# Turning normed tokens by VectorE pieces and DRAM transfers in place of TensorE identity products, in an adaLN + S4 convolution + SwiGLU kernel

## The chip, the cores and the metric

The kernel runs on one core of a Trainium2 chip. The metric is device time in microseconds (us), the median of several runs. One execution is also recorded by the hardware profiler; its rows are what this document calls the profile or the trace, and its times count from the first instruction of that execution.

The core has five engines that each work through their own list of instructions in order: TensorE (PE in the rows; PEld is its weight load), VectorE (DVE), ScalarE (ACT), GpSimd (POOL) and SyncE (SP, which here only issues DMAs). They wait for one another by semaphores. SBUF is the on-chip memory, PSUM the memory that matmuls write.

## The reference, cut to what matters

Input: 2048 tokens of width D = 448, as 16 tiles of 128 tokens.

```python
sa, ca, ga, sb, cb, gb = (silu(c) @ w_mod).reshape(6, D)
h = layernorm(x) * (1 + ca) + sa
x = x + ga * (S4_convolution(h) + h * Dskip)      # along the tokens
h = layernorm(x) * (1 + cb) + sb
x = x + gb * ((silu(h @ w_gate) * (h @ w_up)) @ w_down)   # inner width 1792
```

All of it is in float32. The second layernorm, its modulation by cb and sb, and the fact that `h @ w_gate` contracts over the 448 features are what the change touches: tokens lie on the partitions when they are normed, and features must lie on the partitions when they are multiplied.

## The kernel before, in words

The tokens are taken in six blocks of 2, 2, 3, 3, 3 and 3 tiles (BLOCKS, line 26). `run_blocks` (line 662 on) goes through them; for each it calls `ffn` (line 664), which runs 14 steps f = 0 to 13, one for each 128 of the 1792 inner columns. In a step:

- `gate_up(f)` (line 669) does 22 matmuls in two groups of 11 (line 686): the gate product into one PSUM bank, the up product into the next. Each group takes seven products with `hhi` and four with `hlo`. These two tiles hold the normed, modulated and turned tokens as a rounded part and a residual, in four slices k of 128 features (the fourth repeats the last 64). ScalarE then takes the silu of the first bank (line 701), VectorE multiplies (line 714), ScalarE casts the product to `phi` (line 717) and VectorE takes the residual `plo` (line 718).
- `down(f - 1)` (line 722) follows on TensorE, nine matmuls for three tiles and six for two (line 730), into the PSUM banks `dn`. So a step's product is needed one whole step later.

The banks of `gate_up` come from a ring of four (`bank()`, line 72), which the scan products below use too.

While a block is in its 14 steps, the tiles of the next block are prepared inside them. Every step has two places, early (after `gate_up`, before `down`) and late (after `down`), so half-step h means step h // 2, late if h is odd. `TIMES` (lines 32 to 36) gives by hand the half-steps for each tile: first entry for the first block, second for the second, last for all others. On VectorE, ScalarE and GpSimd there is nothing of `down`, so on them only h // 2 counts, and the order within a step is that of the list. The stages of a tile (`small_path`, line 808 on) are:

- s0: first norm and modulation (lines 184, 186), VectorE; s1: two products v0, v1 (line 824), on VectorE in the second block, on GpSimd from the third on.
- s2: the running sums of the tile before are added into one row of v0 (line 829, VectorE) and of v1 (line 830, VectorE in the second block, else GpSimd); then vh, a cast on ScalarE (line 837), and vl, its residual on VectorE (line 838). s3: h times gd (line 843), engine as s1.
- s4: three matmuls with `tri` (lines 849 to 851), a cumulative sum over the tile's tokens, in the order vh, v1, vl; and an addition into x (line 852). s5: the running sums leave (lines 873 to 875, with a small DMA issued by ScalarE) and x is finished (lines 876, 877).

After its last stage come the second norm's statistics (`stat`, lines 148 and 149), then, once for all tiles of the block, `root` on GpSimd (lines 165 to 172, four operations), then `make_xn` on ScalarE for each tile (line 199, two instructions of 448 and 64 columns) into buffers `xn_of`, which lie in staging space that the weights no longer need.

In step 13, after `gate_up(13)` and ahead of `down(12)`, `transposes` (line 201) turns the tiles: for each slice k, one matmul with the identity per tile into a PSUM bank (line 206), then the splits. ScalarE writes hhi with the modulation (line 207); ScalarE (odd k, line 209) or VectorE (even k, line 211) writes the modulated value back in place; VectorE writes hlo (line 212). Then `down(12)` and `down(13)` run, and `gate_up(0)` of the next block needs hhi and hlo. After a block, VectorE multiplies `dn` by gb into a buffer (line 757), adds it to x (line 758), and SP stores x (line 759) and loads the tiles of the block after next (line 86).

Of the kernel before, what the change touches and what calls it, by code (L numbers as in the profile page):

```python
# [16 lines left out]
L, D, N, F = 2048, 448, 256, 1792  # L17
# [13 lines left out]

TIMES = (
# [3 lines left out]
)  # L36

EXTRA = (1,)
# [14 lines left out]
def f32(ap):  # L53
    return ap.bitcast(F32)
# [3 lines left out]
def tile_kernel(ctx, tc, x, a_re, a_im, b_re, b_im, c_re, c_im, log_dt, dskip,  # L58
# [29 lines left out]


    wgu, raw, wdn, wp = {}, {}, {}, {}  # L90
    stage = [const.tile([128, 2, 4, 128], F32, name=f"raw{q}") for q in range(NS)]
    stage_d = [const.tile([128, D], F32, name=f"rawd{q}") for q in range(NS)]

    xbuf += stage_d[0:2 * MB - 4]
    spare = [t.rearrange("p a b c -> p (a b c)") for t in stage]
    xn_of = [spare[2][:, 0:512], spare[2][:, 512:1024], spare[0][:, 0:512]]
    p_of = [spare[1][:, q * 512:q * 512 + MB * 128] for q in range(2)]

    def load_w(pool, j):
        wgu[j] = pool.tile([128, 2, 7, 128], F32R, name=f"gu{j}")  # L100
# [100 lines left out]
    def transposes(ts):  # L201
        n = len(ts) * 128
        for k in range(4):
# [7 lines left out]
                ve.tensor_scalar(ps[:, 0:n], ps[:, 0:n], cb1c[:, k:k + 1], sbc[:, k:k + 1], op0=OP.mult, op1=OP.add)  # L211
            ve.tensor_tensor(hlo[:, k, 0:n], ps[:, 0:n], f32(hhi[:, k, 0:n]), op=OP.subtract)


    wp0 = ctx.enter_context(tc.tile_pool(name="wp0", bufs=1))
    ones = const.tile([128, 1], F32)
# [445 lines left out]
    def run_blocks(pools, stages, first=None):  # L662
        work, hid = pools.work, pools.hid
        def ffn(ts, fresh, last, todo):
            n = len(ts) * 128
            dn, pp = [], {}
            qz = [(q, z) for z in range(3) for q in range(len(ts))]

            def gate_up(f, nw):
                head = fresh and f == 0  # L670
                if fresh and f > 1:
                    split_d(f)
                w = wgu[f]
                p = hid.tile([128, 256], F32, name="p") if fresh else p_of[f % 2]
                hi = hid.tile([128, MB * 128], F32R, name="phi")
                lo = hid.tile([128, MB * 128], F32R, name="plo")
                ps = [DN[2] if head else bank(), bank()]

                top = [(k, a) for k, ws in enumerate(((0, 4), (1, 5), (2, 6), (3,))) for a in ws]
                low = [(k, k) for k in range(4)]

                def mm(s, ka, lo, first=False, end=False):
                    for q, (k, a) in enumerate(ka):
                        pe.matmul(ps[s][:, 0:n], w[:, s, a], (hlo if lo else hhi)[:, k, 0:n],  # L686
                                  start=first and q == 0, stop=end and q == len(ka) - 1)

                if head:
                    for k in range(3):  # L690
                        for s in range(2):
                            mm(s, [(k, k)], False, k == 0)
                    for s in range(2):
                        mm(s, [(k, 4 + k) for k in range(3)] + [(3, 3)], False)
                    for s in range(2):
                        mm(s, low, True, False, True)
                else:
                    for s in range(2):
                        mm(s, top, False, True)
                        mm(s, low, True, False, True)  # L700
                sc.activation(p[:, 0:n], ps[0][:, 0:n], AF.Silu)  # L701
                pp[f] = hi, lo
                if last and f == NF - 1:
                    c_ = [slice(q * 128, (q + 1) * 128) for q in range(len(ts))]
                    for q in range(len(ts) + 1):
                        for o in c_[q:q + 1]:
                            ve.tensor_tensor(ps[1][:, o], p[:, o], ps[1][:, o], op=OP.mult)
                            sc.copy(hi[:, o], ps[1][:, o])
                        for o in c_[max(q - 1, 0):q]:
                            ve.tensor_tensor(lo[:, o], ps[1][:, o], f32(hi[:, o]), op=OP.subtract)  # L710
                    return
                if nw is not None:
                    split_w(nw, 0)
                ve.tensor_tensor(ps[1][:, 0:n], p[:, 0:n], ps[1][:, 0:n], op=OP.mult)  # L714
                if nw is not None:
                    split_w(nw, 1)
                sc.copy(hi[:, 0:n], ps[1][:, 0:n])  # L717
                ve.tensor_tensor(lo[:, 0:n], ps[1][:, 0:n], f32(hi[:, 0:n]), op=OP.subtract)  # L718
                if nw is not None:
                    split_w(nw, 2)  # L720

            def down(f, qz):
                if not dn:
                    dn.extend(DN[q] for q in range(len(ts)))
                hi, lo = pp[f]
                wh, wl = wp[f]
                for q, z in qz:
                    cs = slice(q * 128, (q + 1) * 128)
                    u, v = ((hi, wh), (hi, wl), (lo, wh))[z]
                    pe.matmul(dn[q][:, 0:D], u[:, cs], v, start=f == 0 and z == 0, stop=f == NF - 1 and z == 2)  # L730

            for f in range(NF):
                gate_up(f, f + 2 if fresh and f and f + 2 < NF else None)
                if fresh:
                    pools.load(f + 2 + NS if f else NF, f + NS)
                for g, a in todo.get((f, 0), []):
                    g(*a)
                if f and not (last and f == NF - 1):
                    down(f - 1, qz)
                for g, a in todo.get((f, 1), []):  # L740
                    g(*a)
            if not last:
                down(NF - 1, qz)
            m = len(ts) - 1
            for q, i in enumerate(ts):
                t = xn_of[q][:, 0:D]
                if last:
                    down(NF - 2, [(e, z) for e in ((0, 1) if q == 0 else range(q + 1, min(q + 2, m + 1))) for z in range(3)])
                    down(NF - 1, [(q, z) for z in range(3)])

                if last and q == m:
                    for a, e, dma in ((0, 256, sc), (256, D, sy)):
                        ve.tensor_tensor(dn[q][:, a:e], dn[q][:, a:e], gb[:, a:e], op=OP.mult)
                        ve.tensor_tensor(xs[i][:, a:e], dn[q][:, a:e], xs[i][:, a:e], op=OP.add)
                        dma.dma_start(out[i * 128:(i + 1) * 128, a:e], xs[i][:, a:e])
                    continue
                ve.tensor_tensor(t, dn[q][:, 0:D], gb, op=OP.mult)  # L757
                (po if last and q else ve).tensor_tensor(xs[i], xs[i], t, op=OP.add)  # L758
                sy.dma_start(out[i * 128:(i + 1) * 128, :], xs[i])
# [13 lines left out]
        for b, ts in enumerate(TILES):  # L773
            todo = {}
            if b + 1 < len(TILES):
                nx = TILES[b + 1]

                def at(f, late, g, *a):
                    todo.setdefault((f, late), []).append((g, a))

                if b:
                    for i in nx:
                        at(0, 1, load_x, i)
                stat1, root1, times, root2, shift = TIMES[min(b, 2)]
                st = stages(b)

                def go(h, g, *a):
                    at(h // 2, h % 2, g, *a)

                if b == 0 and first is None:  # L790
                    go(EXTRA[0], gate_0)
                for i, h in zip(nx, stat1):
                    go(h, n1.stat, i, nx)
                go(root1, n1.root, nx)

                for h, q, z in sorted((h, q, z) for q, hs in enumerate(times) for z, h in enumerate(hs)):
                    if z < len(times[q]) - 1:
                        if z < len(st):
                            go(h, st[z], nx[q])
                    else:  # L800
                        go(h, n2.stat, nx[q], nx)
                go(root2, n2.root, nx)
                for q, (h, i) in enumerate(zip(shift, nx)):
                    go(h, make_xn, i, xn_of[q])
                at(NF - 1, 0, transposes, nx)
            ffn(ts, b == 0, b + 1 == len(TILES), todo)

    def small_path(pools):
# [175 lines left out]
```

## Time and profile before

| | us |
|---|---|
| median of 3 runs | 493.64 (493.01 to 493.94) |
| profiled execution, first to last instruction | 491.7 |
| median of the runs less that span | 1.9 |
| TensorE busy | 482.0 |
| VectorE busy | 265.9 |
| ScalarE busy | 161.3 |
| GpSimd busy | 70.3 |

The mean granted TensorE clock of the execution is 0.995. By the timeline, the first block's 14 steps begin near 39 us, the second block's at 98.9, the third's at 155.2, the fourth's at 238.2, the fifth's at 321 and the last one's at 404.

A row of the timeline has the start in us, the length in us, the engine, the line of the kernel, the operation, output and inputs by the program's names, shapes and how many instructions were merged into the row; in brackets the engine's idle time before it and what ended it. A letter q behind an engine (SPq) marks its sequencer, which issues DMAs. A row of a group gives, behind the bar, the total busy time in us, the mean length in ns, and the idle time before. Buffers are named by the tile they were first allocated as: `raw` is the staging space, so `raw<-x` at line 199 is make_xn. In the rows for DMAs the last number is the median time from issue to landing.

### The profile page before, as it was taken

The numbers are of one execution on the slowest core, as the hardware profiler recorded it, in microseconds if no ns is written. First come the engines' busy times: TensorE is split into PE (matmuls) and PEld (weight loads), VectorE is DVE, ScalarE is ACT, GpSimd is POOL, SyncE is SP. The second block draws the span as 40 slices with busy tenths as digits, with TensorE's granted clock in tenths as the row PEclk, the third lists the DMA queues.
The fourth block names the chain that finished last, engine by engine and source line by source line (L and its number), as shares of the span: only waits on it lengthen the run. The fifth ranks groups of instructions, "written<-read, shape, count | busy, mean of one in ns | idle before, by whom it ended". The sixth has DMA issues, their size and how long they took to land.

```text
span 491.7 us, 6939 instructions
## 1 busy us (share of the span) xinstructions
PE 482.0 (98%) x2759; PEld 452.5 (92%) x2759; DVE 265.9 (54%) x516; ACT 161.3 (33%) x348; POOL 70.3 (14%) x92
## 2 busy tenths in 40 slices
PE   8999999999999999999999999999999999999993
PEld 5659988999999999999999999999999999999992
DVE  4868999568886445634735553473465353221113
ACT  5665555622226112224412222521222161111110
POOL 2241001000010032411006140101541100000000
PEclk9999999999999999999999999999999999999998
DMA  8944752020000200000300000030000001000001
GB/s 309 404 165 159 232 188 86 15 95 1 0 3 21 75 1 0 2 1 2 98 15 1 2 0 2 2 112 1 0 2 1 1 0 57 0 1 0 1 0 64
DMA packets 11979, 26.04 MB, mean 53 GB/s; under 512 B 1825, under 2 KB 7842, under 8 KB 11938
## 3 DMA queue, kind: packets, MB, share of 16 engines
q1 hardware_dynamic: 11232, 25.33, 14.9%
q8 instruction: 23, 0.38, 0.3%
q10 hardware_dynamic: 706, 0.18, 0.2%
q14 instruction: 18, 0.15, 0.1%
HBM read 21.80 MB, written 3.67 MB: 52 GB/s over the span
## 4 chain that ended last, share of the span: by engine, by line
PE 97%; DVE 1%; ACT 0%; issue 0%; POOL 0%; POOLq 0%; DVEq 0%
PE bank L686 58%; PE dn L730 27%; PE bank L225 2%; PE bank L241 1%; PE bank L206 1%; PE dn L420 1%; PE bank L229 1%; PE cv L851 0%; PE cv L849 0%; PE bank L850 0%; PE cv L225 0%; PE bank L376 0%; PE bank L863 0%; PE cv L206 0%; PE cv L864 0%; PE dn L310 0%
## 5 line engine op out<-in xcount | busy, mean ns | idle before, releaser
L686 PE MATMUL bank<-hhi,gu 128*128 128x384 f32 (+1 forms) x1169 | 210.2, 319 | 0.0
L686 PEld LDWEIGHTS bank<-hhi,gu 128*128 128x128 f32 x1169 | 190.4, 188 | 3.1 <-issue 0.7
L686 PE MATMUL bank<-hlo,gu 128*128 128x384 f32 (+1 forms) x668 | 131.6, 319 | 0.0
L714 DVE TENSOR_TENSOR bank<-raw,bank 128x384 f32<-128x384 f32 (+1 forms) x69 | 36.9, 534 | 144.0 <-PE bank L686 128.6
L686 PEld LDWEIGHTS bank<-hlo,gu 128*128 128x128 f32 x668 | 109.7, 188 | 0.1
L717 ACT CAST phi<-bank 128x384 fp32r<-128x384 f32 (+1 forms) x83 | 36.8, 444 | 145.2 <-DVE bank L714 145.2
L701 ACT ACTIVATE raw<-bank 128x384 f32<-128x384 f32 (+1 forms) x70 | 32.8, 469 | 121.8 <-PE bank L686 115.4
L718 DVE TENSOR_TENSOR plo<-bank,phi 128x384 fp32r<-128x384 f32 (+1 forms) x83 | 42.5, 512 | 37.5 <-ACT phi L717 37.5
L730 PE MATMUL dn<-wdh,phi 128*128 128x448 f32 x224 | 60.4, 368 | 0.0
L730 PE MATMUL dn<-wdh,plo 128*128 128x448 f32 x224 | 60.2, 367 | 0.1
L730 PE MATMUL dn<-wdl,phi 128*128 128x448 f32 x224 | 59.9, 366 | 0.0
L730 PEld LDWEIGHTS dn<-wdh,plo 128*128 128x128 f32 x224 | 42.1, 188 | 3.9 <-DVE plo L710 0.4
L730 PEld LDWEIGHTS dn<-wdl,phi 128*128 128x128 f32 x224 | 42.1, 188 | 3.6
L730 PEld LDWEIGHTS dn<-wdh,phi 128*128 128x128 f32 x224 | 39.6, 188 | 1.7 <-ACT run L873 0.7
L824 POOL TENSOR_TENSOR m<-m,gm 128x448 f32<-128x448 f32 x9 | 11.1, 1237 | 64.9 <-DVE m L186 55.3
L165 POOL TENSOR_SCALAR rsb<-mvb 128x3 f32<-128x3 f32 (+2 forms) x7 | 1.9, 272 | 120.4 <-DVE mvb L149 120.4
L165 POOL TENSOR_SCALAR rsa<-mva 128x3 f32<-128x3 f32 (+1 forms) x6 | 1.4, 229 | 105.9 <-DVE mva L149 105.9
L120 ACT CAST gu<-raw 128x1024 fp32r<-128x1024 f32 x14 | 14.6, 1044 | 0.0
L758 POOL TENSOR_TENSOR x<-x,raw 128x448 f32<-128x448 f32 x1 | 1.1, 1129 | 91.2 <-DVE raw L757 91.2
L837 ACT CAST vh<-m 128x448 fp32r<-128x448 f32 x12 | 6.8, 567 | 22.3 <-DVE m L829 22.3
L830 POOL TENSOR_TENSOR v<-v,run 1x448 fp32r<-1x448 f32 x9 | 11.4, 1269 | 17.8 <-DMA run<-run 17.5
L225 PE MATMUL bank<-wm,cs 128*128 128x448 f32 x30 | 12.6, 550 | 0.0
(196 smaller groups left out, 426.8 us busy)
## 6 DMA issues: line engine op xcount, KB each, us to landing
raw<-in_B_w_gate_up_dram SPq DMA_DIRECT2D x14, 512.0 KB, 3.8
rawd<-in_B_w_down_dram SPq DMA_DIRECT2D x14, 224.0 KB, 3.9
x<-in_A_u_dram SPq DMA_DIRECT2D x12, 224.0 KB, 2.8
out_dram<-x SPq DMA_DIRECT2D x11, 224.0 KB, 1.9
wm<-in_w_mod_groups_dram SPq DMA_DIRECT2D x5, 448.0 KB, 8.1
wm<-in_w_mod_groups_dram SPq DMA_DIRECT2D x5, 336.0 KB, 7.9
rawd<-in_A_u_dram SPq DMA_DIRECT2D x4, 224.0 KB, 3.3
out_dram<-rawd SPq DMA_DIRECT2D x4, 224.0 KB, 1.9
```

Source lines behind the costliest of these rows:

```text
L120: sc.copy(wgu[j][:, :, 0:4, :], w)
L206: pe.transpose(ps[:, j * 128:(j + 1) * 128], xn[i][:, k * 128:(k + 1) * 128], ident)
L225: pe.matmul(ps[:, 0:D], cs[:, k:k + 1].to_broadcast([128, 128]), w[:, k * D:(k + 1) * D], start=k == 0, stop=False)
L686: pe.matmul(ps[s][:, 0:n], w[:, s, a], (hlo if lo else hhi)[:, k, 0:n], start=first and q == 0, stop=end and q == len(ka) - 1)
L701: sc.activation(p[:, 0:n], ps[0][:, 0:n], AF.Silu)
L714: ve.tensor_tensor(ps[1][:, 0:n], p[:, 0:n], ps[1][:, 0:n], op=OP.mult)
L717: sc.copy(hi[:, 0:n], ps[1][:, 0:n])
L718: ve.tensor_tensor(lo[:, 0:n], ps[1][:, 0:n], f32(hi[:, 0:n]), op=OP.subtract)
L730: pe.matmul(dn[q][:, 0:D], u[:, cs], v, start=f == 0 and z == 0, stop=f == NF - 1 and z == 2)
L824: (ve if on_v else po).tensor_tensor(v, h, g, op=OP.mult)
L830: (ve if on_v else po).tensor_tensor(v1[0:1], f32(v1[0:1]), run1[0:1], op=OP.add)
L837: sc.copy(vh, v0)
```

## The change

For the tiles of the third block and later (those that are prepared while the second to fifth block run), the identity products are gone. Each tile is turned by itself, soon after its own norm:

- `root` and `make_xn` run tile by tile: `stat` and `root` at a tile's last half-step h, `make_xn` at h + 1, the new `turn` at h + 2.
- `turn`: VectorE transposes the 128 x 512 tile in 32x32 pieces into the neighbouring buffer, SP writes that to DRAM (256 KB), and four reads issued by SP bring it back, one to each group of 32 partitions, in runs of 128 elements, so that features lie on the partitions.
- In step 13, `split_turned` does the same splits as before, with SBUF in place of PSUM as source, taking for each slice k the pieces of all tiles, which lie 128 elements apart in one buffer.
- `TIMES` is changed: in the second block tile one's s3 and tile two's s2 to s5 move one or two half-steps earlier; from the third block on all stages are one half-step earlier.
- The three staging tiles become one, cut into slices; `p_of` and `xn_of` move in it. The product of `dn` and gb at the end of a block (line 757) is written back into `dn` rather than into a staging buffer, except in the last block.

The tiles of the second block, prepared during the first, are still turned by `transposes`.

```diff
 TIMES = (
     ((1, 1), 5, ((5, 10, 15, 15, 15), (9, 9, 18, 19, 19)), 19, (24, 23)),
-    ((2, 3, 3), 3, ((5, 6, 8, 10, 10, 11, 13), (7, 8, 14, 15, 17, 17, 18), (13, 17, 17, 18, 20, 21, 21)), 25, (25, 25, 25)),
-    ((3, 3, 3), 4, ((6, 7, 9, 10, 11, 12, 13), (8, 9, 14, 15, 16, 17, 18), (12, 13, 19, 19, 21, 22, 22)), 23, (24, 24, 25)),
+    ((2, 3, 3), 3, ((5, 6, 8, 9, 10, 11, 12), (7, 8, 13, 14, 15, 16, 17), (12, 16, 18, 18, 20, 21, 21))),
+    ((2, 3, 3), 3, ((5, 6, 8, 9, 10, 11, 12), (7, 8, 13, 14, 15, 16, 17), (11, 12, 18, 18, 20, 21, 21))),
 )
...
-    stage = [const.tile([128, 2, 4, 128], F32, name=f"raw{q}") for q in range(NS)]
+    stages_ = const.tile([128, NS, 2, 4, 128], F32, name="raw")
+    stage = [stages_[:, q] for q in range(NS)]
...
+    spare = stages_.rearrange("p q a b c -> p (q a b c)")
+    tb = spare[:, 1024:3072]
+    xn_of = [tb[:, 1024:1536], tb[:, 1536:2048]]
+    t_of = [tb[:, q * 512:(q + 1) * 512] for q in range(MB + 1)]
+    turned = tb[:, 0:MB * 512].rearrange("p (q a k r) -> p q a k r", q=MB, a=4, k=4)
...
+    xd = [dram.tile([128, 512], F32, name=f"xd{q}") for q in range(MB)]
+
+    def turn(i, q):
+
+        src, dst = t_of[q], t_of[q + 1]
+        ve.transpose(dst.rearrange("p (b k r) -> p k b r", b=4, k=4), src.rearrange("p (k b c) -> p k b c", b=4, k=4))
+        sy.dma_start(xd[q], dst)
+        for b in range(4):
+            sy.dma_start(src[b * 32:(b + 1) * 32].rearrange("c (a n) -> c a n", a=4),
+                         xd[q][:, b * 128:(b + 1) * 128].rearrange("(a c) n -> c a n", a=4))
+
+    def split_turned(ts):
+        n, m = len(ts) * 128, len(ts)
+        for k in range(4):
+            t = turned[:, 0:m, :, k, :]
+            hi, lo = (h[:, k, 0:n].rearrange("p (q a r) -> p q a r", q=m, a=4) for h in (hhi, hlo))
+            sc.activation(hi, t, AF.Identity, scale=cb1c[:, k:k + 1], bias=sbc[:, k:k + 1])
+            if k % 2:
+                sc.activation(t, t, AF.Identity, scale=cb1c[:, k:k + 1], bias=sbc[:, k:k + 1])
+            else:
+                ve.tensor_scalar(t, t, cb1c[:, k:k + 1], sbc[:, k:k + 1], op0=OP.mult, op1=OP.add)
+            ve.tensor_tensor(lo, t, f32(hi), op=OP.subtract)
...
-                t = xn_of[q][:, 0:D]
...
+                t = t_of[q][:, 0:D] if last else dn[q][:, 0:D]
                 ve.tensor_tensor(t, dn[q][:, 0:D], gb, op=OP.mult)
...
+                    elif b == 0:
+                        go(h, n2.stat, nx[q], nx)
                     else:
-                        go(h, n2.stat, nx[q], nx)
-                go(root2, n2.root, nx)
-                for q, (h, i) in enumerate(zip(shift, nx)):
-                    go(h, make_xn, i, xn_of[q])
-                at(NF - 1, 0, transposes, nx)
+                        i = nx[q]
+                        go(h, n2.stat, i, [i])
+                        go(h, n2.root, [i])
+                        go(h + 1, make_xn, i, t_of[q])
+                        go(h + 2, turn, i, q)
...
+                at(NF - 1, 0, split_turned if b else transposes, nx)
```

In the prediction the three tiles of a block that is being prepared are called tile one, two and three, and "block two" is the block during whose steps the third block's tiles are prepared.

More of the change, by code (lines that the diff above doesn't have):

```diff
@@ L90, in tile_kernel @@
     wgu, raw, wdn, wp = {}, {}, {}, {}
-    stage = [const.tile([128, 2, 4, 128], F32, name=f"raw{q}") for q in range(NS)]
+    stages_ = const.tile([128, NS, 2, 4, 128], F32, name="raw")
+    stage = [stages_[:, q] for q in range(NS)]
     stage_d = [const.tile([128, D], F32, name=f"rawd{q}") for q in range(NS)]
     xbuf += stage_d[0:2 * MB - 4]
-    spare = [t.rearrange("p a b c -> p (a b c)") for t in stage]
-    xn_of = [spare[2][:, 0:512], spare[2][:, 512:1024], spare[0][:, 0:512]]
-    p_of = [spare[1][:, q * 512:q * 512 + MB * 128] for q in range(2)]
+    spare = stages_.rearrange("p q a b c -> p (q a b c)")
[3 more added lines that the diff above has]
+    turned = tb[:, 0:MB * 512].rearrange("p (q a k r) -> p q a k r", q=MB, a=4, k=4)
+    p_of = [spare[:, q * 512:q * 512 + MB * 128] for q in range(2)]
     def load_w(pool, j):
@@ L783, in run_blocks @@
                         at(0, 1, load_x, i)
-                stat1, root1, times, root2, shift = TIMES[min(b, 2)]
+                stat1, root1, times = TIMES[min(b, 2)][0:3]
                 st = stages(b)
@@ L799, in run_blocks @@
                             go(h, st[z], nx[q])
-                    else:
-                        go(h, n2.stat, nx[q], nx)
-                go(root2, n2.root, nx)
-                for q, (h, i) in enumerate(zip(shift, nx)):
-                    go(h, make_xn, i, xn_of[q])
-                at(NF - 1, 0, transposes, nx)
+                    elif b == 0:
+                        go(h, n2.stat, nx[q], nx)
+                    else:
+                        i = nx[q]
[3 more added lines that the diff above has]
+                        go(h + 2, turn, i, q)
+                if b == 0:
+                    root2, shift = TIMES[0][3:]
+                    go(root2, n2.root, nx)
+                    for q, (h, i) in enumerate(zip(shift, nx)):
+                        go(h, make_xn, i, xn_of[q])
+                at(NF - 1, 0, split_turned if b else transposes, nx)
             ffn(ts, b == 0, b + 1 == len(TILES), todo)
```

## The prediction, made before the changed kernel had run

> **What bounds the kernel now.** I read the page first: the span, then the chain that ended last.
>
> ```profile
> span 491.7 us, 6939 instructions
> ...
> PE 97%; DVE 1%; ACT 0%; issue 0%; POOL 0%; POOLq 0%; DVEq 0%
> ```
>
> TensorE sets the end: only matmuls taken off it, or waits put into it, move the time. The rest of the working is about which other engine could come to hold it. So next I read busy time by window, one inside the second block (two tiles, 256 tokens) and one of the same length inside the third (three tiles, 384 tokens); the columns are PE, PEld, DVE, ACT, POOL, granted clock, DMA share, GB/s.
>
> ```profile
> 110.00:146.00 36.00, 36.00 (x263) 34.90 (x262) 30.40 (x60) 10.05 (x25) 1.13 (x3) 1.00 0.01 1
> 193.00:229.00 36.00, 36.00 (x197) 35.05 (x196) 19.62 (x36) 9.13 (x19) 9.06 (x10) 1.00 0.01 1
> ```
>
> TensorE is full in both, at full clock. VectorE is not the same in both: 30.4 of 36 us in the second block (84%), 19.6 (54%) in the third. The second block prepares the third block's three tiles inside 14 shorter steps, and its scan stages run on VectorE rather than GpSimd. This asymmetry decides my forecast: what is added to VectorE has room in blocks three to five and hardly any in block two.
>
> Third, the boundary between the third and fourth block, by timeline: TensorE, then the first and last of the splits.
>
> ```profile
> 233.23 0.82 PE L206 MATMUL bank<-ident,raw 128*128 128x128 f32 x6
> ...
> 234.46 0.84 PE L730 MATMUL dn<-wdh,phi 128*128 128x448 f32 x3
> ...
> 238.18 1.40 PE L686 MATMUL bank<-hhi,gu 128*128 128x384 f32 x7
> 239.41 0.87 PE L686 MATMUL bank<-hlo,gu 128*128 128x384 f32 x4
> ```
>
> ```profile
> 234.47 1.24 ACT L207 ACTIVATE hhi<-bank,sbc,cb1c 128x384 fp32r<-128x384 f32 x2
> ```
>
> ```profile
> 238.07 0.55 DVE L212 TENSOR_TENSOR hlo<-bank,hhi 128x384 fp32r<-128x384 f32 x1
> ```
>
> Twelve identity products hold TensorE from 233.23 to 234.46, **1.23 us**. The new block's first product starts at 238.18, its seven hhi products take 1.23 (0.176 each), and its eleventh, on the last hlo, starts 10 x 0.176 = 1.76 after the first, at 239.94. The last hlo is ready at 238.62: 1.3 us of slack, which is all of what the removal may use.
>
> **The change, part by part.** Removed: 1.23 us of TensorE at each of four boundaries, 4.9 us if all of it is kept.
>
> *Blocks three to five, boundary.* Without the products TensorE wants the last hlo at 239.94 - 1.23 = 238.71. The splits start no earlier, because ScalarE takes them behind the last cast of the old block. Their input is now SBUF, not PSUM.
>
> ```profile
> L207 ACT ACTIVATE hhi<-bank,sbc,cb1c 128x384 fp32r<-128x384 f32 x12 | 7.7, 682 | 0.0
> L199 ACT ACTIVATE raw<-x,ngb,rsb 128x448 f32<-128x448 f32 x10 | 7.6, 756 | 0.0
> ```
>
> The SBUF-fed form takes 74 ns more for 64 columns more, so one instruction costs 0 to 0.07 us extra; I take 0.04, which is 0.2 over the six in a row. The last hlo is then ready at 238.82: 0.1 us of wait, gain 1.13.
>
> *Blocks three to five, schedule.* The new TIMES move the second tile's products with tri (s4) from step 8 to step 7 late, and each tile gets a root of its own on GpSimd. These rows are of the third block.
>
> ```profile
> 193.49 0.56 DVE L718 TENSOR_TENSOR plo<-bank,phi 128x384 fp32r<-128x384 f32 x1 [0.55 <-ACT phi L717]
> ...
> 200.97 0.82 DVE L838 TENSOR_TENSOR vl<-m,vh 128x448 fp32r<-128x448 f32 x1 [0.69 <-ACT vh L837]
> ```
>
> ```profile
> 198.66 1.15 POOL L824 TENSOR_TENSOR v<-m,g 128x448 fp32r<-128x448 f32 x1
> 199.76 1.53 POOL L830 TENSOR_TENSOR v<-v,run 1x448 fp32r<-1x448 f32 x1
> ```
>
> ```profile
> 199.63 1.40 PE L686 MATMUL bank<-hhi,gu 128*128 128x384 f32 x7
> ...
> 203.51 0.36 PE L849 MATMUL cv<-vh,tri 128*128 128x448 f32 x1
> ```
>
> The second norm's root in the second block, first and last of its four operations:
>
> ```profile
> 145.66 0.23 POOL L165 TENSOR_SCALAR rsb<-mvb 128x3 f32<-128x3 f32 x1 [34.77 <-DVE mvb L149]
> ...
> 147.22 0.26 POOL L172 TENSOR_SCALAR ngb<-ngb 128x3 f32<-128x3 f32 x1
> ```
>
> s4 ran at 203.51; now it is due at 199.63, after down of step 6, and its second product, on v1, at 199.83. GpSimd's order in step 6 is root of tile one, s1 of tile three (two operations), then the addition into v1 of tile two. The statistics follow the plo of 193.49 and end about 194.7; a root takes 1.82 us (145.66 to 147.48), s1 2 x 1.15, the addition 1.15, and one of these runs beside a VectorE operation on two SBUF tiles and takes 1.53. That is v1 at 200.3: a **wait of 0.45** (from 0, if the root is faster, to 1.2, if all three are slow). Net per block: 1.13 - 0.45 = 0.68, three blocks **-2.0 us**.
>
> *Block two.* Here the three turns, three roots and three make_xn enter VectorE's full order. Spacings are taken from these rows.
>
> ```profile
> 122.25 0.63 DVE L874 SCALAR_TENSOR_TENSOR run<-run,cv 32x448 f32<-32x448 f32 x1
> ...
> 124.17 0.42 DVE L714 TENSOR_TENSOR bank<-raw,bank 128x256 f32<-128x256 f32 x1
> ...
> 125.37 0.62 DVE L148 BATCH_NORM_STATS2 stb<-rawd 128x6 f32<-128x448 f32 x1
> ...
> 126.11 0.65 DVE L184 SCALAR_TENSOR_TENSOR m<-x,mva,ca 128x448 f32<-128x448 f32 x1
> ...
> 127.70 0.43 DVE L714 TENSOR_TENSOR bank<-raw,bank 128x256 f32<-128x256 f32 x1 [0.21 <-PE bank L686]
> ...
> 130.14 0.63 DVE L838 TENSOR_TENSOR vl<-m,vh 128x448 fp32r<-128x448 f32 x1
> 130.68 0.62 DVE L843 TENSOR_TENSOR m<-m,gd 128x448 f32<-128x448 f32 x1
> ```
>
> ```profile
> 129.54 0.57 ACT L837 CAST vh<-m 128x448 fp32r<-128x448 f32 x1 [1.01 <-DVE m L829]
> ...
> 148.67 2.08 ACT L199 ACTIVATE raw<-rawd,ngb,rsb 128x448 f32<-128x448 f32 x4
> 150.65 1.08 ACT L199 ACTIVATE raw<-x,ngb,rsb 128x448 f32<-128x448 f32 x2
> ```
>
> So: s5's three operations 1.92; a step's product, cast and residual 1.20; statistics 0.74; s0 1.38 (1.59 less the 0.21 wait); any one 448-wide operation 0.54; make_xn 0.99 a tile; vh 0.6 with its release. No row shows the turn: one pass over 512 columns, and 448 take 0.62 and 256 take 0.42, so 0.68 long and 0.62 apart; the low bound is a narrower pass, 0.42, the high bound two passes, 1.24. I take the one that continues the rows.
>
> The Trainium skill, "VectorE: DVE Perf Modes", section "The three transpose paths", gives 311 ns for 128x128 bf16 on VectorE against 390 ns on TensorE, and its rules for kernel authors still leave a full 128x128 turn on TensorE. Four such VectorE pieces make 1.24 us, an estimate from that page; by it the forecast would be 1.7 us later (three turns, 0.56 more each). The trace shows TensorE at 1.23/12 = 0.10 us each in a stream, against the page's 390 ns: what is removed is cheap.
>
> VectorE from the step-6 product, unchanged at 124.17, as all that precedes it is only reordered: step 6 to 125.4; statistics of tile one 126.1; s0 of tile three 127.5; two row additions 128.6. Then vl of tile two **waits**: its vh sits on ScalarE behind make_xn of tile one, which waits for the root (126.2 + 1.82 = 128.0, make_xn 129.0, vh 129.6). vl 130.15; step 7 131.35; turn 132.0; s3 and the addition into x 133.2; step 8 134.4; s5 136.4; s1 of tile three 137.5; statistics 138.2; step 9 139.4; row additions 140.5; vl of tile three **waits again** (root 140.2, make_xn 141.2, vh 141.8) to 142.3; s3 and turn 143.5; step 10 144.7; addition and s5 147.2; statistics 147.95; root 149.9; make_xn 150.9; **last turn done 151.65**. Queued behind each waiting vl are the next step's product and residual, and behind vh its silu; TensorE itself waits in s4 for vh and vl (about 1.1 for tile two, 0.4 for tile three), and about 1.0 for a bank that s5 frees late.
>
> Then the transfers.
>
> ```profile
> x<-in_A_u_dram SPq DMA_DIRECT2D x12, 224.0 KB, 2.8
> out_dram<-x SPq DMA_DIRECT2D x11, 224.0 KB, 1.9
> ```
>
> ```profile
> 102.74 0.87 SPq L86 DMA_DIRECT2D rawd<-in_A_u_dram  x2
> ```
>
> Nothing else is on SP's queue there. The 256 KB write takes 1.9 to 2.1, I take 2.0: 153.7. The four reads wait for it, are issued 0.44 apart, and land 1.9 to 2.8 after issue; I take 2.2: 153.7 + 1.3 + 2.2 = **157.2**. All splits need all tiles.
>
> ```profile
> 152.76 1.24 ACT L207 ACTIVATE hhi<-bank,sbc,cb1c 128x384 fp32r<-128x384 f32 x2
> ```
>
> ```profile
> 156.35 0.55 DVE L212 TENSOR_TENSOR hlo<-bank,hhi 128x384 fp32r<-128x384 f32 x1
> ```
>
> The splits began at 152.76 and the last hlo was ready at 156.90, which TensorE already waited for. Now they begin at 157.2 and, with 0.2 for SBUF, end at 161.5: **+4.6 us** (4.44 + 0.2). TensorE's own waits of 2.5 do not add to this: it would come to the new block here,
>
> ```profile
> 155.21 1.40 PE L686 MATMUL bank<-hhi,gu 128*128 128x384 f32 x7
> ```
>
> less 1.23, plus 2.5, at 156.5, ahead of the data. So the 1.23 removed there is lost in the wait, and the end is set by VectorE's order and the transfers.
>
> *The turn in blocks three to five* hides. Its last one stands behind this plo of step 11 and one make_xn:
>
> ```profile
> 223.19 0.56 DVE L718 TENSOR_TENSOR plo<-bank,phi 128x384 fp32r<-128x384 f32 x1 [0.55 <-ACT phi L717]
> ```
>
> That is a turn done near 225 and, with the same 5.5 us of transfers, data near 230.5, four before the splits at 234.47. If this cover went, the lateness would stand in the path, as in block two.
>
> Small edits at nothing: dn times gb in place in PSUM (needed again only after two gate products of 3.88, as 199.63 to 203.51 shows one), the joined staging buffer.
>
> Sum: 491.7 + 4.6 - 2.0 = 494.3, **+2.6 us**. The runs' median of 493.64 lies 1.9 above this span; on it, 496.2.
>
> **The rivals.** *Forecast: late turn in block two,* +1 to +5, chance 0.58. Its own range, 494.6 to 498.6, comes from the turn (each 0.1 us more is 0.3 at the end), the transfers (-0.8 to +0.7), and v1's wait (three times -0.45 to +0.75).
>
> *Short roots, faster.* The three roots of block two stand in the path with two vl waits (2.2) and the last root itself (1.95 from statistics to make_xn), and once in each later block (3 x 0.45): 5.5 us in all. A one-tile root of 0.5 us in place of 1.82 would give back about 4.0, so -1.4: 492.2. It decides from a root of 0.97 us, where the sum is zero. Against it stands the one-tile form of a single one of its four operations, from the first block:
>
> ```profile
> L166 POOL TENSOR_TENSOR rsb<-rsb,mhalf 128x1 f32<-128x1 f32 x2 | 1.6, 790 | 0.2
> ```
>
> Chance 0.12.
>
> *A draw.* The low ends together: transfers of 1.9 + 1.0 + 1.9 (-0.7) and no wait on v1 (-1.35) leave +0.5, 494.1. Chance 0.17.
>
> *Costlier splits or turns, slower still.* The four slices that the splits take lie interleaved in one buffer. If each split is made to wait for the one before it on the other engine, the chain of 4.1 us (152.76 to 156.90) grows by about one 0.55-us residual twice, +1 at each of four boundaries; or the turn takes two passes, +1.7: 498 to 501. Chance 0.13.
>
> Faster by over 0.2% (1 us, about what a measurement here can tell from no change) 0.12, within 0.17, slower 0.71. The range leaves out half of the faster rival and the far half of the costlier one: 492.6 to 500.2.
>
> **What would show it.** Right: in block two a DVE vl that waits about 1 us for vh, twice; last turn ending near 151.7; reads landing near 157; ScalarE idle for a DMA before its first split, TensorE idle 3 us or more there and L206 at 8 products only; in blocks three to five a period shorter by 0.5 to 1.1. Wrong: no TensorE gap at that first boundary (then the VectorE sum is too long), a turn over 1 us, splits spaced much over 0.6, or s4 without a wait in blocks three to five.

## The result, and the profile after

The changed kernel takes **502.31 us** in the median of five runs (500.27 to 503.73), against 493.64 (493.01 to 494.65) in five runs of the kernel before: ratio 1.0173, 95% interval 1.0156 to 1.0189. The sign of the forecast was right; its size was not, and 502.31 lies above the range's 500.2. The profiled execution is the shortest of the five (500.27, span 498.4). Its page, first line and chain:

```profile
span 498.4 us, 7008 instructions
...
PE 79%; DVE 8%; ACT 5%; POOL 4%; issue 2%; DMA 1%; SPq 0%; ACTq 0%; DVEq 0%; POOLq 0%
```

Where TensorE held 97% of the chain, it now holds 79%: for 17% of the span DVE, ACT and POOL held the end. The view of TensorE's waits from 98 us on names them (total us, times, longest). In the kernel before that view is empty.

```profile
PE cv L884 <- ACT vh L872: 3.4, 2, 1.7
PE bank L713 <- ACT hhi L235: 2.5, 2, 1.8
PE bank L885 <- POOL v L865: 1.2, 3, 0.4
PE bank L713 <- DVE hlo L240: 1.1, 4, 0.4
```

To place the loss I use one mark per block, the first `down`, and the time from mark to mark. The timeline of TensorE before:

```profile
104.02 0.57 PE L730 MATMUL dn<-wdh,phi 128*128 128x448 f32 x2
...
162.96 0.78 PE L730 MATMUL dn<-wdh,phi 128*128 128x448 f32 x3
...
245.94 0.77 PE L730 MATMUL dn<-wdh,phi 128*128 128x448 f32 x3
```

and after, with the waits in between:

```profile
104.01 0.57 PE L757 MATMUL dn<-wdh,phi 128*128 128x448 f32 x2
...
130.45 0.47 PE L884 MATMUL cv<-vh,tri 128*128 128x448 f32 x1 [1.65 <-ACT vh L872]
...
143.47 0.47 PE L884 MATMUL cv<-vh,tri 128*128 128x448 f32 x1 [1.72 <-ACT vh L872]
...
160.26 1.22 PE L713 MATMUL bank<-hhi,gu 128*128 128x384 f32 x4 [1.83 <-ACT hhi L235]
162.20 1.04 PE L713 MATMUL bank<-hhi,gu 128*128 128x384 f32 x3 [0.72 <-ACT hhi L235]
...
164.13 0.44 PE L713 MATMUL bank<-hlo,gu 128*128 128x384 f32 x1 [0.38 <-DVE hlo L240]
...
170.13 0.78 PE L757 MATMUL dn<-wdh,phi 128*128 128x448 f32 x3
...
206.81 0.37 PE L884 MATMUL cv<-vh,tri 128*128 128x448 f32 x1
207.56 0.47 PE L885 MATMUL bank<-v,tri 128*128 128x448 f32 x1 [0.39 <-POOL v L865]
...
246.85 0.45 PE L713 MATMUL bank<-hlo,gu 128*128 128x384 f32 x1 [0.23 <-DVE hlo L240]
...
252.86 0.78 PE L757 MATMUL dn<-wdh,phi 128*128 128x448 f32 x3
```

**Block two** took 58.94 us (104.02 to 162.96) and now takes 66.12: +7.18. **Block three** took 82.98 and now takes 82.73; the next two gained 0.14 and 0.12 (marks at 335.57 and 418.30 after, 328.79 and 411.64 before). So 1.23 us per boundary was removed, and only 0.51 was kept in three later blocks together, where the prediction had 2.0. 7.18 less 0.51 is the 6.7 us between the two spans.

### The profile page after: what moved, and what is told of

It is laid out like the page before. It is cut to its first block, busy times and chain, and to the rows that moved or that the text cites. A ratio compares the mean times of both kernels' runs of the same rounds, so it can differ in the third digit from the quotient of the medians.

```text
span 498.4 us, 7008 instructions
## 1 busy us (share of the span) xinstructions
PE 480.7 (96%) x2711; PEld 446.6 (90%) x2711; DVE 276.1 (55%) x528; ACT 163.2 (33%) x348; POOL 78.2 (16%) x124
## 4 chain that ended last, share of the span: by engine, by line
PE 79%; DVE 8%; ACT 5%; POOL 4%; issue 2%; DMA 1%; SPq 0%; ACTq 0%; DVEq 0%; POOLq 0%
PE bank L713 49%; PE dn L757 19%; PE bank L252 2%; ACT hhi L235 2%; DVE bank L741 1%; ACT raw L237 1%; PE bank L268 1%; DMA rawd<-in_A_u_dram 1%; POOL v L865 1%; PE dn L447 1%; ACT phi L744 1%; PE bank L256 1%; DVE plo L745 1%; POOL v L859 1%; POOL m L859 1%
## 5 line engine op out<-in xcount | busy, mean ns | idle before, releaser
L169 POOL TENSOR_SCALAR rsb<-mvb 128x1 f32<-128x1 f32 (+1 forms) x15 | 4.8, 318 | 163.4 <-DVE mvb L153 163.4
L873 DVE TENSOR_TENSOR vl<-m,vh 128x448 fp32r<-128x448 f32 x12 | 8.9, 742 | 16.5 <-ACT vh L872 16.4
L203 ACT ACTIVATE raw<-x,ngb,rsb 128x448 f32<-128x448 f32 (+1 forms) x20 | 10.9, 596 | 7.3 <-POOL ngb L176 7.3
```

Of the source, the lines that this page charges most:

```text
L203: sc.activation(xn[i][:, o:o + n], src[:, a:a + n], AF.Identity, scale=rs, bias=ng)
L873: ve.tensor_tensor(vl, v0, f32(vh), op=OP.subtract)
```

## What the waits in block two are made of

The first wait, followed on three engines of the changed kernel: GpSimd's root of tile one, what ScalarE does behind it, and VectorE.

```profile
126.16 0.57 POOL L169 TENSOR_SCALAR rsb<-mvb 128x1 f32<-128x1 f32 x1 [15.44 <-DVE mvb L153]
126.81 0.99 POOL L170 TENSOR_TENSOR rsb<-rsb,mhalf 128x1 f32<-128x1 f32 x1
127.88 0.60 POOL L175 TENSOR_TENSOR ngb<-mvb,rsb 128x1 f32<-128x1 f32 x1
128.57 0.25 POOL L176 TENSOR_SCALAR ngb<-ngb 128x1 f32<-128x1 f32 x1
```

```profile
128.85 1.09 ACT L203 ACTIVATE raw<-rawd,ngb,rsb 128x448 f32<-128x448 f32 x2 [3.99 <-POOL ngb L176]
129.85 0.55 ACT L872 CAST vh<-m 128x448 fp32r<-128x448 f32 x1
```

```profile
130.43 0.63 DVE L873 TENSOR_TENSOR vl<-m,vh 128x448 fp32r<-128x448 f32 x1 [2.01 <-ACT vh L872]
...
152.71 0.71 DVE L224 STREAM_TRANSPOSE raw<-raw 128x512 f32<-128x512 f32 x1 [1.57 <-ACT raw L203]
```

The chain is the one that the prediction drew: root, make_xn, then vh, which waits in ScalarE's order for a root that it has no use for. But the root took 2.66 us (126.16 to 128.82), not 1.82; the second took 2.19 (139.65 to 141.84) and the third 1.47 (150.08 to 151.55). The last turn ends at 153.42 (predicted 151.65). Behind it, SP's issues and ScalarE's first split:

```profile
153.45 0.34 SPq L225 DMA_DIRECT2D xd<-raw  x1
155.60 1.73 SPq L227 DMA_DIRECT2D raw<-xd  x4
```

```profile
159.50 1.31 ACT L235 ACTIVATE hhi<-raw,sbc,cb1c 128x384 fp32r<-128x384 f32 x2 [2.60 <-DMA raw<-xd]
```

From the end of the turn to the first split 6.1 us pass, of which the prediction had 5.5. ScalarE waits for the DMA, and TensorE for ScalarE. The last residual, for which TensorE waits once more, is ready at 164.08:

```profile
163.52 0.56 DVE L240 TENSOR_TENSOR hlo<-raw,hhi 128x384 fp32r<-128x384 f32 x1 [0.27 <-ACT raw L237]
```

One change of places was not named ahead of the result: in the second entry of `TIMES` the third tile's s2 (row additions, vh, vl) moves from half-step 17 to 18, which is one step later, while its s4 stays at 20.

## The experiments

**Theory:** block two makes the whole loss, in two parts: the new order (a cast and three products behind a root), and the trip (turn and transfers) whose cover is used up. Later blocks are a little faster, and their missing gain stands in the waits for v1 and for hlo. **Rivals:** turns or transfers cost wherever they are; one of the two parts of block two costs all.

A third matter came from the runs' list. Spans and mean granted clocks of the changed kernel in its first five runs: 498.4 at 0.996, 499.2 at 0.994, 500.4, 501.3 and 501.9 at 0.988. The kernel before has 0.994 to 0.998 in all of its runs beside the experiments, and spans of 491.0 to 492.4.

### The change from the fourth block on

```diff
+                old = b < 2
-                at(NF - 1, 0, split_turned if b else transposes, nx)
+                at(NF - 1, 0, transposes if old else split_turned, nx)
```

and the old second line of TIMES with it.

> The third block's tokens go the old way (TensorE's identity products, block two's old places), the fourth to sixth blocks' the new way. Theory (the loss is made in block two alone, where the turned tokens come 7.1 us late; blocks three to five win 0.13 us each): span 491.3, time 493.2, ratio 0.999, granted clock 0.995 and a spread of the times under 1.5 us as before. Rival (turns and transfers cost wherever they stand, or pull the clock down): at least half of the loss stays, time 497 or more, spread over 3 us.

Measured: 493.46 us (11 runs, 493.12 to 493.86; before 493.52), ratio 1.000, interval 0.9991 to 1.0009; span 491.6, clocks 0.994 to 0.997. TensorE's waits from 98 us on:

```profile
PE bank L886 <- POOL v L866: 1.1, 3, 0.4
PE bank L713 <- DVE hlo L240: 0.8, 3, 0.3
```

The whole loss and the whole spread are gone, and three turned blocks with all of their DMAs neither cost nor gain anything that can be measured. The rival falls: turns and transfers are hidden in blocks three to five.

### The change in the third block's tokens alone

```diff
+                old = b != 1
```

> Only the third block's tokens go the new way, the later blocks' the old way. Theory (loss in block two alone): the last low-part product of block three's first gate_up starts 7.1 us later than before, span 498.8 in a run at clock 0.996, median time near 502.5 because the clock falls to 0.988 in most runs as it did with the whole change. Rival (loss spread over blocks): span near 493.5, time 495.4, clock 0.995.

Measured: 502.70 us (501.81 to 503.72), ratio 1.0183 (1.0169 to 1.0198), against 502.5 expected. The median is as forecast, but block two took 67.79, not 66.1, in the run that was profiled, and only two of the five runs have a clock below 0.990 (0.987 to 0.995). One at 0.995 still has a span of 500.3, so the mean clock is not all that lengthens a run. The windows of the profiled run show why its block two was longer (the columns are the stretch, its length, TensorE's busy time with its instructions, the granted clock, the DMA share and GB/s):

```profile
128.00:130.30 2.30, 0.74 (x4) 1.00 0.00 0
130.30:132.00 1.70, 1.63 (x8) 0.88 0.00 0
132.00:134.00 2.00, 2.00 (x11) 0.50 0.17 67
134.00:136.00 2.00, 2.00 (x13) 0.75 0.19 70
136.00:140.00 4.00, 4.00 (x31) 1.00 0.25 66
```

TensorE idles 1.63 us before 130.37, starts again at full clock, and a microsecond later runs at **half clock** for about 3.5 us. From the `down` at 127.34 to the next at 135.46 it took 8.12 us, where the whole change's profiled run, with the same wait and clock 1.00, took 6.58 (127.41 to 133.99). A busy TensorE hides this: its busy share is full in these rows, and only the clock column tells. Behind the second wait for vh (1.76) the clock falls again, to 0.58 and 0.59 from 144.90 to 149.00. That stretch hardly moves the end: TensorE then only waits less for the first split at the boundary, 0.43 instead of 1.83.

### The cast ahead of the normalization

```diff
-                        go(h + 1, make_xn, i, t_of[q])
+                        late.append((h + 1, make_xn, i, t_of[q]))
...
+                for e in late:
+                    go(*e)
```

> The whole change, but at the place where both stand, a tile's normalization on ScalarE (which waits for GpSimd's root) is issued behind the other tile's cast to vh instead of ahead of it. Theory (3.4 of block two's 7.1 us are two waits of TensorE for vh, because the cast stands behind a normalization that waits for a root of 2.2 to 2.7 us; the other 3.7 are the trip): both waits vanish, the last low-part product starts 3.4 us earlier, at 160.7, span 495.0 at clock 0.996. Rival (the trip alone sets the end of block two): start and span unchanged, 164.1 and 498.4.

Measured: 499.81 us (498.89 to 500.60), ratio 1.0125 (1.0110 to 1.0141), span 498.0 with a clock of 0.989. TensorE's timeline and, behind it, the windows:

```profile
141.19 0.47 PE L887 MATMUL cv<-vh,tri 128*128 128x448 f32 x1 [1.43 <-ACT vh L875]
...
158.17 1.21 PE L713 MATMUL bank<-hhi,gu 128*128 128x384 f32 x4 [1.99 <-ACT hhi L235]
...
162.53 2.44 PE L713 MATMUL bank<-hhi,gu 128*128 128x384 f32 x7
```

```profile
158.10:160.00 1.90, 1.21 (x4) 0.83 0.00 0
160.00:162.00 2.00, 1.89 (x6) 0.50 0.00 0
162.00:164.00 2.00, 2.00 (x8) 0.50 0.03 8
164.00:166.00 2.00, 2.00 (x8) 0.50 0.67 235
166.00:168.00 2.00, 2.00 (x12) 0.96 0.91 256
```

Of the two waits for vh one is gone; the other stays at 1.43, since there VectorE's row additions are late by themselves (its order is full, and their new place is one step later). The boundary's first product starts 2.1 us earlier (158.17 against 160.26), not 3.4. Then the profiled run gives it back: seven products take 2.44 instead of 1.37 at half clock, and block two ends at 65.96, only 0.16 shorter. A single profile would have said that the order doesn't matter.

### Without the transfers

The write and the four reads of each tile are left out, and the split reads what the turns wrote, so its tokens are turned within pieces only.

```diff
-        sy.dma_start(xd[q], dst)
-        for b in range(4):
-            sy.dma_start(src[b * 32:(b + 1) * 32].rearrange("c (a n) -> c a n", a=4),
-                         xd[q][:, b * 128:(b + 1) * 128].rearrange("(a c) n -> c a n", a=4))
...
-    turned = tb[:, 0:MB * 512].rearrange("p (q a k r) -> p q a k r", q=MB, a=4, k=4)
+    turned = tb[:, 512:(MB + 1) * 512].rearrange("p (q a k r) -> p q a k r", q=MB, a=4, k=4)
```

> The whole change without the transfers through DRAM: this leaves out the write and the four reads of each tile, so that the pieces stay where the turn put them and the product gets tokens that are only turned within pieces. The split reads what the turns wrote. Theory (3.7 of 7.1 us are the trip, 3.4 the two waits for vh): the two waits stay, the boundary has none left, last low-part product at 160.3 to 160.5, span 494.7; blocks three to five unchanged at 82.7 each. Rival (the transfers slow the engines everywhere): blocks three to five get shorter by 0.3 us or more each. Second rival (the late turn alone costs): last product at 162 or later.

Measured: 498.09 us (497.87 to 499.14), ratio 1.0099 (1.0083 to 1.0114), span 496.0. TensorE's waits:

```profile
PE cv L879 <- ACT vh L867: 3.4, 2, 1.7
...
PE bank L708 <- DVE hlo L235: 1.1, 4, 0.4
PE bank L708 <- ACT hhi L230: 0.4, 1, 0.4
```

The two waits for vh stay to the tenth; the boundary's fall from 2.9 to 0.7. Block two takes 63.46 (104.57 to 168.03): the transfers are worth 2.66 of the 7.18, a microsecond less than I had expected. Blocks three to five do not get shorter (82.93, 82.66, 82.68 against 82.73, 82.71, 82.73), so the traffic slows nothing there.

### The new order alone

In block two no turn and no transfer, TensorE's products are back; places, roots and normalizations are the new ones.

```diff
+                        if b > 1:
+                            go(h + 2, turn, i, q)
...
-                at(NF - 1, 0, split_turned if b else transposes, nx)
+                at(NF - 1, 0, split_turned if b > 1 else transposes, nx)
```

> In block two only the order is new (its new places, a root for each tile, each normalization one place behind); its tokens are turned by TensorE's identity products and nothing goes through DRAM. Blocks three to five have the whole change. Theory (the two waits for vh come from the normalization that waits for GpSimd's root ahead of the cast, not from the turn): both waits stay at 1.5 to 1.75 us each, no wait at the boundary, first down of block three 3.4 us later than before relative to block two's first, span 494.8, time 496.7 at clock 0.996. Rival (the turn's own VectorE time makes the waits): waits under 0.5 us, span 491.6.

Measured: 498.20 us (497.89 to 498.32), ratio 1.0090 (1.0075 to 1.0106), span 496.0. The first of TensorE's waits, the only one inside block two:

```profile
PE cv L885 <- ACT vh L873: 3.3, 2, 1.7
```

Both waits stand without any turn on VectorE: they are made by the new order, that is by places, roots and normalizations together (that the places alone would make one of them was not run). Block two takes 63.29, that is **+4.35 for the order alone**, a microsecond more than the waits for vh of 3.3. Most of the rest is in the same two places, where the three products with tri, 0.2 apart when they are fed, stand 0.31 to 0.35 apart (in the changed kernel at 130.45, 130.76 and 131.11, the next at 131.42), the third of them behind vl, which follows vh. Turn and trip then add 66.12 - 63.29 = 2.83, net of the 1.23 that they remove. The span is 1.2 later than I had written, 1.0 of it from this.

### The idle times filled

Matmuls whose result is not used, ahead of the second and third tile's products with tri in block two, and at the boundary behind it:

```diff
+            if i in TILES[2][1:]:
+                fill(8)
             pe.matmul(o, tri, vh, start=True, stop=False)
...
                 down(NF - 1, qz)
+                if ts == TILES[1]:
+                    fill(8)
```

> The whole change, plus matmuls whose result is not used at the three places where TensorE idles in and behind block two: eight of 128x512 ahead of the second and third tile's products with tri there (waits of 1.65 and 1.72 us), and eight at the boundary behind it (1.83). Theory (what lifts the median 2 us over the profiled run is a granted clock of 0.50 for a few us behind such idle times, in some runs and not in others): every run at clock 0.995 or more, spans 498.0 to 499.0, median time 500.4, spread under 1.5 us. Rival (the lower clock has another source): clocks of 0.988 and a median of 502.3 as without the filling, or later by what the filling takes.

Measured: 500.60 us (four runs, 499.99 to 501.49), clocks 0.995 to 0.998, spans 498.2 to 499.7. TensorE's timeline at the first of the three places:

```profile
129.55 2.02 PE L274 MATMUL cv<-tri 128*128 128x512 f32 x8
131.41 0.42 PE L894 MATMUL cv<-vh,tri 128*128 128x448 f32 x1
```

Work was added, and the median is 1.7 us lower than in the five runs of the changed kernel. The profiled run has full clock in and behind block two; 0.9 of the 1.3 by which its span (499.7) is longer than the 498.4 of the changed kernel stands ahead of the first mark (104.90 against 104.01), so a part of the spread has nothing to do with these waits. The changed kernel once more, on another occasion:

> The changed kernel once more, for more runs of it beside the next one. Theory (the low clock comes in some runs only, behind idle times of 1.6 to 2 us of TensorE): runs at clock 0.994 or more have spans of 498.2 to 499.5, runs at 0.990 or less of 500 to 502; in a run with a low clock the granted clock is 0.50 for a few us behind one of the three idle times in and behind block two and 1.00 elsewhere. Rival (a slower chip or engines): the whole run is slower, no stretch of it stands out.

Measured: 501.62 us (500.09 to 503.31; before 493.52), ratio 1.0167 (1.0145 to 1.0189), spans 498.2 at clock 0.997, 498.3 at 0.996, 499.8 and 499.9 at 0.991, 501.4 at 0.985. The bounds of 0.990 and 500 were missed by the middle two, but the order is the same: over its ten runs the span rises, on the whole, as the clock falls, from 498.2 to 501.9. Seven of the ten have a clock below 0.995, and no filled run has. The execution profiled here was again one at full clock, so of this kernel itself no stretch at half clock is on record; it is shown in the two relatives above. Against these five runs the filling gains 1.0 us in the median, with ranges that overlap (500.09 to 503.31 against 499.99 to 501.49). And the repaired order with fillers (six ahead of the third tile's products, nine at the boundary):

> The cast to vh ahead of the normalization, as in the earlier run with that order, plus matmuls whose result is not used at the two places where TensorE still idled there: six of 128x512 ahead of the third tile's products with tri (wait of 1.43 us) and nine at the boundary behind block two (1.99). Theory (that run lost 1.9 us to products at clock 0.50 behind these waits): block two 64.0 us from first down to first down, every run at clock 0.994 or more, span 496.1 to 496.6, median time 498.1. Rival (the gain of the order is small by itself): 65.5 or more, median 499.8.

Measured: 498.80 us (four runs, 498.08 to 499.33), clocks 0.995 and 0.996, profiled span 496.3, block two 64.16 (expected 64.0). Without the fillers the same order took 65.96 in its profile and 499.81 in the median. So the order's gain is real, 66.12 - 64.16 = 1.96, and the half clock had hidden it.

The Trainium skill, "TensorE: Matmul & The Clock Gate", section "Part 1: The HAM clock gate (the "warmup" mystery)", describes a halved TensorE clock behind an idle window of about 3.4 us and full clock again behind a busy one of that length, with windows that run freely. The half rate and the length of the stretches (about 3.5 and twice that) agree; the condition is softer here, since one wait of 1.63 us, or one of 1.99 with one of 0.73 behind it, was enough in some executions.

### Where the later blocks' gain went

From the fourth block on only, with the modulation applied in place one place before the end:

```diff
-            sc.activation(hi, t, AF.Identity, scale=cb1c[:, k:k + 1], bias=sbc[:, k:k + 1])
...
+            sc.copy(hi, t)
             ve.tensor_tensor(lo, t, f32(hi), op=OP.subtract)
...
+                    go(25, modulate, nx)
```

where `modulate` is `tensor_scalar` on VectorE for each k.

> Third block's tokens the old way; from the fourth block on the new way, and the scale and shift are applied to the turned tokens in place by VectorE at the place before the last, so that only the cast to hhi (ScalarE) and the subtraction to hlo (VectorE) stand at the boundary. Theory (in blocks three to five 0.4 us of the 1.23 removed goes to the last hlo, behind six activations 0.65 apart): the wait for hlo of 0.23 and its 0.15 to 0.2 of delay vanish three times, span 490.4, time 492.3. Rival (VectorE's four new operations, 0.48 each, delay the old block's last products): span 491.6 or more.

Measured: 493.14 us (11 runs, 492.18 to 493.97; before 493.67), ratio 0.9989 (0.9980 to 0.9998). The profiled run has the span of 490.4, but it is among the shortest; the median shows 0.5 of the 1.4 expected. Blocks four and five take 82.28 and 82.26, 0.45 less than with the whole change; block three takes 83.05, with a new wait, of the old block's `down` for phi (0.51): there VectorE waits for the reads before it modulates, and the old block's last product stands behind it. That the landing of the reads makes the spread is likely, not shown.

With the third tile's gates one place earlier besides:

```diff
-    ((2, 3, 3), 3, (...), (...), (11, 12, 18, 18, 20, 21, 21))),
+    ((2, 3, 3), 3, (...), (...), (11, 11, 18, 18, 20, 21, 21))),
```

> As the run before, and besides the third tile's two products with the gates on GpSimd stand one place earlier, ahead of the first tile's root instead of behind it. Theory (0.55 us of the 1.23 goes to the addition into v1, which waits on GpSimd behind root and gates): the wait of 0.4 for v1 vanishes three times too, span 488.7, time 490.6. Rival (the root, now later, moves the turn into the path, or the wait passes to vl on VectorE): span 490.4 or more.

Measured: **490.61 us** (490.38 to 491.47; before 493.67), ratio 0.9943 (0.9929 to 0.9956), span 488.7: faster than both kernels. Its chain, and TensorE's waits from 98 us on, all of them:

```profile
PE 96%; DVE 2%; DMA 0%; ACT 0%; issue 0%; SPq 0%; POOL 0%; DVEq 0%; POOLq 0%
```

```profile
PE dn L758 <- ACT phi L745: 0.2, 1, 0.2
```

Blocks four and five take 81.62 and 81.63, against 82.85 before: 1.23 less, all that the identity products had cost. So the change kept 0.13 there because the last hlo took 0.45 (82.72 to 82.27) and v1 the other 0.64.

## Why the prediction was wrong in size

The forecast misses the result by 6.1 us (502.31 - 496.2). By its own steps:

- **Removed, 1.23 us at each boundary:** right; the last version gets just that.
- **The turn, 0.68:** right, one pass:

```profile
L224 DVE STREAM_TRANSPOSE raw<-raw x12: 700/705/711, 132.2 to 397.4; 128x512 f32<-128x512 f32 x12
```

  The 1.24 that the prediction worked out beside it from the Trainium skill, "VectorE: DVE Perf Modes", section "The three transpose paths", would have been too long by 0.54 a turn.
- **Turn and transfers hidden in blocks three to five:** right, shown by the run from the fourth block on.
- **Boundary and v1 in blocks three to five, net 0.68 each:** wrong, 0.17 each, **1.5 us** of the miss. Mechanisms and places are right, both terms too small. The wait for hlo costs 0.45, not 0.1. The prediction took the extra of an SBUF-fed split from the lengths of single instructions, and these differ little (0.695 against 0.682); the starts differ more. The six activations of the splits now stand 0.66 apart on average, where those from PSUM stood 0.56 apart (234.47 to 237.26 in the kernel before):

```profile
242.21 1.31 ACT L235 ACTIVATE hhi<-raw,sbc,cb1c 128x384 fp32r<-128x384 f32 x2
...
245.50 0.71 ACT L237 ACTIVATE raw<-raw,sbc,cb1c 128x384 f32<-128x384 f32 x1
```

  And v1 costs 0.64, not 0.45. The wait itself is as predicted: TensorE was due at 207.01, 0.2 behind the product on vh, and GpSimd's addition ends at 207.50.

```profile
205.98 1.52 POOL L865 TENSOR_TENSOR v<-v,run 1x448 fp32r<-1x448 f32 x1
```

  What was left out is the restart: the product starts 0.06 behind that, and the next one 0.31 behind it instead of 0.2.
- **Block two, +4.6:** the mechanism is right (vl behind vh behind make_xn behind a root, twice; then last turn, transfers, splits, boundary), its size is 7.18: **2.6 us** of the miss. On the prediction's own path the last hlo was to be ready at 161.5, and it was at 164.08. Of these 2.6 us, 1.8 stand at the end of the last turn (153.42 for 151.65), 0.6 in the transfers (6.1 for 5.5) and 0.3 in the splits (4.6 for 4.3). Half of the 1.8 is the one-tile root, put at 1.82 three times: it took 2.66, then 2.19 and 1.47, together 0.9 more. The other half was added between the roots, in VectorE's order. TensorE's own waits, 2.5 in the prediction, are 4.35 by the order-only run, so they were too small as well; that they are hidden, because the data come later still, held. The bank wait of 1.0 among them isn't in the trace.
- **Run to run:** the step that is not in the prediction at all. It set the profiled span plus 1.9 equal to the median, as holds for the kernel before. After the change the median lies **2.0 us** above the profiled run, the shortest of its five. By the medians, 1.0 to 1.7 of it go when TensorE's idle times are filled, behind some of which its clock is halved; the remainder stays open. The prediction counted a wait of TensorE at its own length, where in one profile 1.63 us of wait brought 1.54 more.
- **Rivals:** no split waits for another's slice, and roots are not short. The faster rival's point stands, though: its mechanism, the roots, was one of the largest errors, to the other side.

## What to carry to other kernels

A fused step that is cut into one per tile puts several short waits of a slow engine into the order of faster ones; ask for each instruction that now stands behind it (here a cast that fed TensorE) whether it needs it, and put it ahead if not. Price a wait of an engine that sets the end by more than its length where it may drop that engine's clock, and read the clock column beside the busy time, over several runs. And removed work is only gained when all the other waits at the same place have slack as well: here two waits, worth 0.45 and 0.64, took back all but 0.13 of a 1.23.

## What the runs showed of the hardware

- TensorE ran at half clock for about 3.5 to 7 us behind waits of 1.6 to 2.0 us, in some executions and not in others with the same waits; the mean clock of the changed kernel went from 0.985 to 0.997 over ten runs.
- GpSimd's 128x1 power operation took 0.99 us beside two VectorE operations on SBUF operands and 0.57 elsewhere in block two; the whole four-operation root went from 2.66 to 1.47. The Trainium skill, "GPSIMD Engine Reference", section "1. Specifications", has GpSimd share its SBUF interfaces with VectorE where that takes two SBUF inputs, which agrees; no run here isolates it.
- A plain cast on ScalarE from SBUF, 128x384, ran about 0.42 apart (four in 1.75 us, 0.51 each), where the activations with scale and bias on the same source ran 0.66 apart (the six from 242.21 to 245.50, 0.70 each).
